# Transposing the attention output by DMA instead of TensorE in a fused attention and feed-forward kernel

## The chip, the cores and the metric

The kernel runs on one core of one Trainium2 chip. The metric is the device time of one execution in microseconds (us); the median over several runs is quoted. The span of an execution, from its first to its last instruction, is 1.7 to 1.8 us shorter than its time, so spans are compared with spans and times with times. TensorE is called PE, VectorE DVE, ScalarE ACT, GpSimd POOL; SP is the sync engine, whose sequencer issues DMAs in program order. PSUM is the memory that PE writes (`psum` in the profile). The granted clock is the share of full speed at which PE is let run. The chain of waits is followed back from the last instruction, at each step to what released it.

## The reference

Attention with a cosine-weighted linear kernel, 8 batches, 8 heads, 576 positions, head size 64. Its output, reordered to 4608 tokens x 512 channels, is the input of a feed-forward layer with a gate (512 to 1536 and back).

```python
def phi(x, c, s):                       # c, s: cos and sin of the position
    r = np.maximum(x, 0.0)
    return np.concatenate([r * c, r * s], axis=-1)
q_p, k_p = phi(q, cos_w, sin_w), phi(k, cos_w, sin_w)
kv  = einsum('bhsf,bhsd->bhfd', k_p, v);   z = sum(k_p, axis=2)
num = einsum('bhsf,bhfd->bhsd', q_p, kv)
den = einsum('bhsf,bhf->bhs', q_p, z)[..., None] + 1e-06
x   = (num / den).transpose(0, 2, 1, 3).reshape(4608, 512)
out = (gelu(x @ w_gate) * (x @ w_val)) @ w_out
```

## The kernel before

PE runs the feed-forward layer in nine blocks of 512 tokens. A block has 12 steps; each does the gate and value matmuls of 128 hidden columns (`gv_unit`, 8 matmuls of 512 columns) and a quarter of an output tile of the block before (`o_step`, 4 matmuls). In blocks 2 to 6 the attention of batch `blk + 1` (3 to 7) is threaded between them. A batch is 576 tokens and a block 512, so batch 3 fills the last 320 tokens of block 3 and the first 256 of block 4, while batch 7 fills only the last 64 of block 7 and all of block 8.

A batch goes through these units: `prep_step` makes the products of relu(q) and relu(k) with cos and sin on DVE, `cast_v` casts v on POOL, `turn_q` transposes the q products by DMA, `kv_unit` is the k-v product on PE, `nm_unit` makes the numerators and denominators of 128 tokens on PE and divides on DVE into `x_sb`, and `xt_unit` transposes that tile on PE and copies it with ACT into `xT`, which `gv_unit` reads as its moving operand. The product of gate and value is written by DVE into `hT`, which the output matmuls read.

```python
def nm_unit(b, t, bank=4):
    c0 = min(t * 128, S - 128)
    ps = psum[:, bank:bank + 2]
    ...                                   # 8 matmuls of 65 columns
    x = attn2.tile([128, 2, 4, D], BF16, name="x_sb")      # pool of 2 buffers
    nc.vector.tensor_scalar_add(den, nm[:, :, :, D], EPS)
    nc.vector.reciprocal(rec, den)
    nc.vector.tensor_tensor(x, nm[:, :, :, 0:D], ..., op=ALU.mult)
    bt[b, t] = x

def xt_unit(b, t, bank=6):
    x = bt.pop((b, t)).rearrange("p g h d -> p (g h d)")
    ps = psum[:, bank, 0:CT * 64].bitcast(BF16).rearrange("p (c n) -> p c n", c=CT)
    for ct in range(CT):                  # CT = 4
        nc.tensor.transpose(
            out=ps[:, ct, :], in_=x[:, ct * 128:(ct + 1) * 128], identity=ident)
    ...
    for blk, c, m in pieces(b * S + t * 128, n):           # a tile may span two blocks
        nc.scalar.copy(xT_block(blk)[:, :, c:c + m], ps[:, :, o:o + m])
        o += m

...
for blk in range(2, 9):
    b = blk + 1
    for jt in range(JT):                  # JT = 12 steps
        gv_unit(BLK * blk, BLK, jt)
        if b < B:
            if jt < 3:
                prep_step("kp", b, jt)
            if 1 <= jt < 5:
                cast_v(b, jt - 1, 1)
            if jt == 5:
                kv_unit(b)
                if b + 1 < B:
                    load_batch(b + 1)     # k, v of b+1 and q of b+2, on the sync queue
            if 6 <= jt < 6 + NT:          # NT = 5 tiles
                nm_unit(b, jt - 6)
            if jt >= 7:
                xt_unit(b, jt - 7)
            if b + 1 < B and jt >= 9:
                prep_step("qp", b + 1, jt - 9)
                if jt == 11:
                    turn_q(b + 1, 0, NP)  # two DMA transposes, on the sync queue
        o_step(blk - 1, jt)               # every third step also stores a tile
```

Of the kernel before, what the change touches and what calls it, by code (L numbers as in the profile page):

```python
# [10 lines left out]
BF16 = mybir.dt.bfloat16  # L11
# [5 lines left out]
def kernel(  # L17
# [14 lines left out]
    nc = tc.nc  # L32

    B, H, S, D = q.shape
# [16 lines left out]
    attn2 = ctx.enter_context(tc.tile_pool(name="attn2", bufs=2))  # L51
# [14 lines left out]
    def rows(t, b):  # L66
        return t[b].rearrange("(m i) (p j) d -> (i p) m (j d)", i=2, j=R)
# [3 lines left out]
    def load(eng, name, src, b, cuts=((0, NP),), j0=0, j1=R):  # L71
        if (name, b) not in staged:
            staged[name, b] = inp.tile(
                [128, NP, R * D], FP32, name=name, bufs=2 if name == "qf" else 1
            )
        js = slice(j0 * D, j1 * D)
        for m, n in cuts:
            eng.dma_start(
                out=staged[name, b][:, m:m + n, js], in_=rows(src, b)[:, m:m + n, js]
            )  # L80
# [48 lines left out]
    for i in range(2):  # L129
        t = consts.tile([128, NP, R, D + 1], BF16, name=f"vx{i}")  # L130
# [48 lines left out]
    def cast_v(b, m=0, n=NP, copy=nc.gpsimd.tensor_copy):  # L179
        copy(  # L180
            vx_tiles[b % 2][:, m:m + n, :, 0:D],
            staged["vf", b][:, m:m + n].rearrange("p m (j d) -> p m j d", j=R),
        )
# [48 lines left out]
    def turn_q(b, pair0, n):  # L232
        qt_tile(b)
        src = phi["qp", b]
        for i in range(2):
            nc.sync.dma_start_transpose(
                out=qT[b][i][:, pair0:pair0 + n].rearrange("f m (j p) -> f (m j) p", p=64),
                in_=src[64 * i:64 * i + 64, pair0:pair0 + n].rearrange(
                    "p m j f -> p (m j f)"
                ),  # L240
            )
# [3 lines left out]
    def kv_unit(b, groups=1):  # L245
        kp, vx = phi["kp", b], vx_tiles[b % 2]
        ps = psum[:, 4:6]
        kv = attn2.tile([128, NP, 2, D + 1], BF16, name="kv_sb")
        psv = ps[:, :, 0:NP * (D + 1)].rearrange("p i (m d) -> p m i d", m=NP)
        per = NP // groups  # L250
        for g in range(groups):
            for pair in range(g * per, (g + 1) * per):
                for j in range(R):
                    for i in range(2):
                        rr = slice(64 * i, 64 * i + 64)
                        nc.tensor.matmul(  # L256
                            psv[:, pair, i],
                            lhsT=kp[rr, pair, j, :],
                            rhs=vx[rr, pair, j, :],
                            start=(j == 0),  # L260
                            stop=(j == R - 1),
                        )
            nc.scalar.copy(kv[:, g * per:(g + 1) * per], psv[:, g * per:(g + 1) * per])
        kv_sb[b] = kv

    bt = {}
# [4 lines that stand above are left out]
        for h in range(H):  # L271
            nc.tensor.matmul(  # L272
                ps[:, h // 4, (h % 4) * (D + 1):(h % 4 + 1) * (D + 1)],
                lhsT=qT[b][h % 2][:, h // 2, c0:c0 + 128],
                rhs=kv_sb[b][:, h // 2, h % 2, :],
                start=True,
                stop=True,
            )
        nm = ps[:, :, 0:4 * (D + 1)].rearrange("p g (h d) -> p g h d", h=4)
        den = attn2.tile([128, 2, 4], FP32, name="den")  # L280
        rec = attn2.tile([128, 2, 4], FP32, name="rec")
        x = attn2.tile([128, 2, 4, D], BF16, name="x_sb")
        nc.vector.tensor_scalar_add(den, nm[:, :, :, D], EPS)
        nc.vector.reciprocal(rec, den)
        nc.vector.tensor_tensor(  # L285
            x,
            nm[:, :, :, 0:D],
            rec[:, :, :, None].to_broadcast([128, 2, 4, D]),
            op=ALU.mult,
        )  # L290
        bt[b, t] = x
# [3 lines left out]
    def xT_block(blk):  # L295
        if blk not in xT:
            xT[blk] = xtp.tile([128, CT, BLK], BF16, name="xT")
        return xT[blk]

    def pieces(c0, n):  # L300

        while n > 0:
            blk = c0 // BLK
            m = min(n, (blk + 1) * BLK - c0)
            yield blk, c0 % BLK, m
            c0, n = c0 + m, n - m
# [4 lines that stand above are left out]
        for ct in range(CT):  # L311
            nc.tensor.transpose(  # L312
                out=ps[:, ct, :], in_=x[:, ct * 128:(ct + 1) * 128], identity=ident
            )
        skip = 128 * (t + 1) - S if 128 * (t + 1) > S else 0
        n = 128 - skip
        o = skip
        for blk, c, m in pieces(b * S + t * 128, n):
            nc.scalar.copy(xT_block(blk)[:, :, c:c + m], ps[:, :, o:o + m])  # L319
            o += m  # L320


# [2 lines left out]
    def gv_unit(c0, n, jt):  # L325
        blk, cc = divmod(c0, BLK)
        xt = xT_block(blk)
        js = slice(jt * 128, (jt + 1) * 128)
        g_ps = next_bank()

        v_ps = g_ps[:, BLK // 2:] if n <= BLK // 2 else next_bank()
        for ps, w in ((g_ps, wg_sb), (v_ps, wv_sb)):
            for ct in range(CT):
                nc.tensor.matmul(  # L334
                    ps[:, 0:n],
                    lhsT=w[:, ct, js],
                    rhs=xt[:, ct, cc:cc + n],
                    start=(ct == 0),
                    stop=(ct == CT - 1),
                )  # L340
        gel = ffn.tile([128, BLK], FP32, name="gel")
        nc.scalar.activation(gel[:, 0:n], g_ps[:, 0:n], AF.Gelu)  # L342
        if blk not in hT:
            hT[blk] = ffn.tile([128, JT, BLK], BF16, name="hT")
        nc.vector.tensor_mul(hT[blk][:, jt, cc:cc + n], gel[:, 0:n], v_ps[:, 0:n])  # L345
# [31 lines left out]


    NT = 5
    def load_batch(b):  # L380
        load(nc.sync, "kf", k, b)
        load(nc.sync, "vf", v, b)
        if b + 1 < B:
            load(nc.sync, "qf", q, b + 1)


    probe = consts.tile([128, 1], FP32)
# [34 lines left out]
    kv_unit(0, 2)  # L422
    keep_warm(8)
    nm_unit(0, 0)
    nm_unit(0, 1, 0)
    keep_warm(8)
    xt_unit(0, 0)
    keep_warm(8)
    xt_unit(0, 1, 7)
    prep("qp", 0, 4, 6)  # L430
    prep("qp", 0, 6, 8)
    for jt in range(8):
        gv_unit(0, 256, jt)
        if jt == 0:
            turn_q_narrow(0, 4, 2)
            prep("qp", 0, 8, R)
        if jt == 1:
            turn_q_narrow(0, 6, 2)
        if jt == 2:
            nm_unit(0, 2)  # L440
        if jt == 3:
            turn_q_narrow(0, 8, 1)
        if jt == 4:
            nm_unit(0, 3)
            xt_unit(0, 2)
        if jt == 6:
            xt_unit(0, 3)
        if jt == 7:
            nm_unit(0, 4)
# [34 lines left out]
    def prep_step(name, b, i):  # L484
        prep(name, b, 3 * i, 3 * i + 3)

    def o_step(blk, i):
        o_part(4 * blk + i // 3, range(4 * (i % 3), 4 * (i % 3) + 4))
# [32 lines left out]
    for jt in range(4, JT):  # L521
# [12 lines left out]
        if jt < 11:  # L534
            o_step(0, jt - 1)
    load(nc.sync, "qf", q, 3)
    load_batch(3)
    nm_unit(2, 4)
    xt_unit(2, 3)
    o_step(0, 10)  # L540
# [6 lines left out]
    for blk in range(2, 9):  # L547
        b = blk + 1
        for jt in range(JT):
            gv_unit(BLK * blk, BLK, jt)  # L550
            if b < B:
                if jt < 3:
                    prep_step("kp", b, jt)
                if 1 <= jt < 5:
                    cast_v(b, jt - 1, 1)
                if jt == 5:
                    kv_unit(b)
                    if b + 1 < B:
                        load_batch(b + 1)
                if 6 <= jt < 6 + NT:  # L560
                    nm_unit(b, jt - 6)
                if jt >= 7:
                    xt_unit(b, jt - 7)
                if b + 1 < B and jt >= 9:
                    prep_step("qp", b + 1, jt - 9)
                    if jt == 11:
                        turn_q(b + 1, 0, NP)
            o_step(blk - 1, jt)
# [49 lines left out]
```

## Time and profile before

| | before |
|---|---|
| time, median of 3 runs | 345.82 us (345.78 to 345.93) |
| span of the profiled execution | 344.4 us |
| PE busy | 94%, granted clock 1.00 in the blocks |
| a block with a batch | 34.85 us |
| a block without | 31.1 us |

Lines of the code that the profile names: L334 gate and value matmuls, L365 output matmuls, L256 k-v, L272 numerators, L312 transposes of x, L319 copies into xT, L236 q transposes, L78 loads, L354 stores.

The page of the kernel before: its span, the busy time of each engine, and the chain of waits by engine and by line.

```profile
span 344.4 us, 6826 instructions
...
PE 324.5 (94%) x2700; PEld 180.9 (53%) x2738; DVE 192.4 (56%) x533; ACT 139.3 (40%) x281; POOL 30.5 (9%) x51
...
PE 88%; DVE 6%; DMA 2%; ACT 1%; issue 1%; SPq 0%; DVEq 0%; ACTq 0%
PE psum L334 52%; PE psum L365 25%; PE psum L256 3%; PE psum L272 3%; PE psum L312 2%; DMA vf<-in_v_dram 2%; DVE kp L148 1%; PE psum L207 1%; DVE x_sb L285 1%; DVE hT L345 1%; PE psum L579 1%; DVE vx_119 L180 1%; ACT xT L319 0%; DVE kp L158
...
L319 ACT COPY xT<-psum 128x512 bf16<-128x512 bf16 (+1 forms) x44 | 21.9, 508 | 24.4 <-PE psum L312 24.3
...
L312 PE MATMUL psum<-ident,x_sb 128*128 128x128 bf16 x160 | 15.5, 219 | 1.7 <-DVE x_sb L285 1.5
```

PE sets the pace of this kernel: it carries 88% of the chain, and the copies of ACT into xT alone waited 24.3 us for PE (the end of the L319 line). The transposes of x have 2.5% of the chain where it is printed with a decimal (2% here). Their 15.5 us "busy" is not what they cost: one is 219 ns long, so 160 of them end to end would be 35.0 us, and four that follow each other have 0.22 us of the chain. What they cost is read from the chain.

The chain in order of time, in the block of batch 4 (columns: start in us, duration in us, what). The k-v product, then steps 6 and 7:

```profile
142.69 1.27 PE psum L256 x72
...
143.96 0.16 issue
144.12 0.81 PE psum L365 x3
144.93 1.73 PE psum L334 x8
146.65 0.26 PE psum L272 x8
146.91 0.86 PE psum L365 x4
147.77 1.73 PE psum L334 x8
149.50 0.26 PE psum L272 x8
149.76 0.22 PE psum L312 x4
149.98 0.22 PE psum L365
```

A step is 1.73 of gate and value matmuls and 0.86 of output matmuls, 2.59 together. Around them stand k-v (1.27, with 0.16 of idle), a numerator (0.26) and a transpose group (0.22). 12 x 2.59 + 1.43 + 5 x (0.26 + 0.22) is 34.9, and the table of windows has 34.85 for the block from one step to the same step of the next block, so nothing else costs PE time there:

```profile
core 0: us, PE busy (x) PEld busy (x) DVE busy (x) ACT busy (x) POOL busy (x), PEclk, DMA share, GB/s
...
131.09:165.94 34.85, 34.48 (x271) 17.64 (x276) 22.37 (x64) 12.81 (x22) 2.50 (x4) 1.00 0.66 167
```

The sync queue at the turn of that block, from the timeline (start, duration, engine, line, operation). The two q transposes hold it for 8.5 us:

```profile
129.64 3.63 SPq L236 DMA_TRANSPOSE qT_2041<-qp  x1
133.36 4.77 SPq L236 DMA_TRANSPOSE qT_2042<-qp  x1
138.23 3.09 SPq L354 DMA_DIRECT2D out_dram<-o_sb  x4
141.41 0.55 SPq L78 DMA_DIRECT2D kf<-in_k_dram  x1
```

### The profile page before, as it was taken

Reading aid. Unit: us, or ns where it says so; the run is one execution under the profiler, and the core shown is the slowest. Engines: PE = TensorE matmul, PEld = TensorE weight load, DVE = VectorE, ACT = ScalarE, POOL = GpSimd, SP = SyncE. Lnnn points to the kernel's source line nnn. Section 1 sums busy time; section 2 is a strip of 40 time slices with the busy share of each in tenths; the row PEclk is TensorE's granted clock in tenths of the full one; section 3 lists DMA queues with packets and bytes.
Section 4 is the critical chain, followed back from the end, with each engine's and each line's share of the span. In section 5 each row is a group of like instructions: output and inputs, shape, how many; then the busy total and the mean of one; then the engine's idle time right before and its main releaser. Section 6 shows DMA issues by size and latency. Waiting matters only on the chain.

```text
span 344.4 us, 6826 instructions
## 1 busy us (share of the span) xinstructions
PE 324.5 (94%) x2700; PEld 180.9 (53%) x2738; DVE 192.4 (56%) x533; ACT 139.3 (40%) x281; POOL 30.5 (9%) x51
## 2 busy tenths in 40 slices
PE   3889998989899999999999999999999999999994
PEld 2778656755445554555455545554555444444443
DVE  5677865994792598258825882588355222322300
ACT  4667955533423443334324433343244333223221
POOL 1831022000200200020002000200000000000000
PEclk9999999999999999999999999999999999999999
DMA  7999984019569807990789079606711111211124
GB/s 285 260 273 305 240 296 163 2 36 371 207 86 237 317 4 107 227 340 0 99 203 370 3 86 216 236 0 92 139 32 33 30 30 38 50 35 30 32 62 91
DMA packets 47888, 48.81 MB, mean 142 GB/s; under 512 B 25200, under 2 KB 33136, under 8 KB 47856
## 3 DMA queue, kind: packets, MB, share of 16 engines
q1 hardware_dynamic: 38000, 34.64, 39.7%
q0 software_dynamic: 8480, 11.80, 14.4%
q10 hardware_dynamic: 1376, 1.93, 1.6%
q8 instruction: 21, 0.34, 0.4%
q14 instruction: 11, 0.09, 0.1%
HBM read 37.75 MB, written 9.44 MB: 137 GB/s over the span
## 4 chain that ended last, share of the span: by engine, by line
PE 88%; DVE 6%; DMA 2%; ACT 1%; issue 1%; SPq 0%; DVEq 0%; ACTq 0%
PE psum L334 52%; PE psum L365 25%; PE psum L256 3%; PE psum L272 3%; PE psum L312 2%; DMA vf<-in_v_dram 2%; DVE kp L148 1%; PE psum L207 1%; DVE x_sb L285 1%; DVE hT L345 1%; PE psum L579 1%; DVE vx_119 L180 1%; ACT xT L319 0%; DVE kp L158 0%; ACT gel L342 0%
## 5 line engine op out<-in xcount | busy, mean ns | idle before, releaser
L345 DVE TENSOR_TENSOR hT<-gel,psum 128x512 bf16<-128x512 f32 (+4 forms) x132 | 77.5, 590 | 127.3 <-PE psum L334 115.1
L342 ACT ACTIVATE gel<-psum 128x512 f32<-128x512 f32 (+4 forms) x132 | 68.5, 520 | 127.7 <-PE psum L334 121.6
L334 PE MATMUL psum<-xT,wg_sb 128*128 128x512 bf16 (+4 forms) x515 | 113.6, 339 | 2.4 <-ACT xT L319 1.4
L334 PE MATMUL psum<-xT,wv_sb 128*128 128x512 bf16 (+4 forms) x516 | 113.2, 339 | 0.6
L365 PE MATMUL psum<-wo_sb,hT 128*128 128x512 bf16 x407 | 104.3, 379 | 1.2 <-issue 0.8
L334 PEld LDWEIGHTS <-wg_sb 128*128 128x128 bf16 x528 | 48.4, 98 | 47.1 <-issue 2.1
L334 PEld LDWEIGHTS <-wv_sb 128*128 128x128 bf16 x528 | 49.0, 98 | 45.4
L365 PEld LDWEIGHTS <-hT 128*128 128x128 bf16 x420 | 38.7, 98 | 39.0
L319 ACT COPY xT<-psum 128x512 bf16<-128x512 bf16 (+1 forms) x44 | 21.9, 508 | 24.4 <-PE psum L312 24.3
L374 ACT COPY o_sb<-psum 128x512 f32<-128x512 f32 x35 | 20.5, 585 | 27.7 <-PE psum L365 26.6
L285 DVE TENSOR_TENSOR x_sb<-psum,rec 128x512 bf16<-128x512 f32 x40 | 27.7, 691 | 1.4
L148 DVE TENSOR_SCALAR qp<-qf,cos_t 128x256 bf16<-128x256 f32 x68 | 23.6, 347 | 0.0
L148 DVE TENSOR_SCALAR kp<-kf,cos_t 128x256 bf16<-128x256 f32 x63 | 21.7, 349 | 0.0
L148 DVE TENSOR_SCALAR qp<-qf,sin_t 128x256 bf16<-128x256 f32 x59 | 20.5, 347 | 0.0
L148 DVE TENSOR_SCALAR kp<-kf,sin_t 128x256 bf16<-128x256 f32 x57 | 20.0, 350 | 0.0
L312 PE MATMUL psum<-ident,x_sb 128*128 128x128 bf16 x160 | 15.5, 219 | 1.7 <-DVE x_sb L285 1.5
L180 POOL CAST vx_121<-vf 128x576 bf16<-128x576 f32 x12 | 7.5, 669 | 96.0 <-DMA vf<-in_v_dram 65.1
L207 PE MATMUL psum<-ident,qp 128*128 128x128 bf16 x108 | 9.2, 232 | 6.3 <-DVE qp L158 5.2
L180 POOL CAST vx_119<-vf 128x576 bf16<-128x576 f32 (+1 forms) x10 | 7.2, 765 | 65.6 <-DMA vf<-in_v_dram 65.6
L256 PEld LDWEIGHTS <-kp 64*128 64x128 bf16 x576 | 10.1, 95 | 5.4 <-issue 3.4
L312 PEld LDWEIGHTS <-x_sb 128*128 128x128 bf16 x160 | 10.0, 97 | 4.7 <-DVE x_sb L285 3.5
L207 PEld LDWEIGHTS <-qp 128*128 128x128 bf16 x108 | 7.3, 103 | 8.3 <-DVE qp L158 6.1
(88 smaller groups left out, 163.5 us busy)
## 6 DMA issues: line engine op xcount, KB each, us to landing
out_dram<-o_sb SPq DMA_DIRECT2D x70, 128.0 KB, 2.4
qf<-in_q_dram SPq DMA_DIRECT2D x5, 1152.0 KB, 11.6
kf<-in_k_dram SPq DMA_DIRECT2D x5, 1152.0 KB, 5.9
vf<-in_v_dram SPq DMA_DIRECT2D x5, 1152.0 KB, 9.2
qf<-in_q_dram POOLq DMA_DIRECT2D x2, 1152.0 KB, 16.3
kf<-in_k_dram POOLq DMA_DIRECT2D x2, 1152.0 KB, 11.4
vf<-in_v_dram POOLq DMA_DIRECT2D x2, 1152.0 KB, 11.8
wo_sb<-in_moe_w_out_dram POOLq DMA_DIRECT2D x2, 768.0 KB, 17.8
```

The costliest lines, as they stand in the source:

```text
L148: nc.vector.tensor_scalar(dst[:, m:m + n, j, part * D:(part + 1) * D], src[:, m:m + n, j], 0.0, (cos_t, sin_t)[part][:, j:j + 1], op0=ALU.max,
L180: copy(vx_tiles[b % 2][:, m:m + n, :, 0:D], staged["vf", b][:, m:m + n].rearrange("p m (j d) -> p m j d", j=R),)
L207: nc.tensor.transpose(out=views[m // per][:, m % per, j], in_=phi["qp", b][:, m, j0 + j, :], identity=ident,)
L256: nc.tensor.matmul(psv[:, pair, i], lhsT=kp[rr, pair, j, :], rhs=vx[rr, pair, j, :], start=(j == 0), stop=(j == R - 1),)
L285: nc.vector.tensor_tensor(x, nm[:, :, :, 0:D], rec[:, :, :, None].to_broadcast([128, 2, 4, D]), op=ALU.mult,)
L312: nc.tensor.transpose(out=ps[:, ct, :], in_=x[:, ct * 128:(ct + 1) * 128], identity=ident)
L319: nc.scalar.copy(xT_block(blk)[:, :, c:c + m], ps[:, :, o:o + m])
L334: nc.tensor.matmul(ps[:, 0:n], lhsT=w[:, ct, js], rhs=xt[:, ct, cc:cc + n], start=(ct == 0), stop=(ct == CT - 1),)
L342: nc.scalar.activation(gel[:, 0:n], g_ps[:, 0:n], AF.Gelu)
L345: nc.vector.tensor_mul(hT[blk][:, jt, cc:cc + n], gel[:, 0:n], v_ps[:, 0:n])
L365: nc.tensor.matmul(o_ps[i], lhsT=hT[blk][:, jt, tt * 128:(tt + 1) * 128], rhs=wo_sb[:, jt, :], start=(jt == 0), stop=(jt == JT - 1),)
L374: nc.scalar.copy(o_sb, o_ps.pop(i))
```

## The change

Its intent: take the 25 transpose groups of batches 3 to 7 off PE, which is the bottleneck, and give them to the DMA engines, which are idle a third of the time in a block with a batch (DMA share 0.66). A DMA takes longer to land (in the kernel before, the q transposes land 6.2 to 8.4 us after their issue, where a group on PE has 0.22 us and a copy into xT 0.51 us in the mean), so k-v and the numerators come one step sooner, there are four x buffers instead of two, and the loads of the next batch are spread over the block instead of being issued together after k-v. Batches 0 to 2 keep PE transposes.

```diff
-        x = attn2.tile([128, 2, 4, D], BF16, name="x_sb")
+        x = attn2.tile([128, 2, 4, D], BF16, name="x_sb", bufs=4)
...
+    def xt_dma(b, t):
+        x = bt.pop((b, t)).rearrange("p g h d -> p (g h d)")
+        o = max(128 * (t + 1) - S, 0)
+        for blk, c, m in pieces(b * S + t * 128, 128 - o):
+            nc.sync.dma_start_transpose(
+                out=xT_block(blk)[:, :, c:c + m], in_=x[o:o + m]
+            )
+            o += m
...
-    load_batch(3)
+    load(nc.sync, "kf", k, 3)
+    load(nc.sync, "vf", v, 3)
...
+                if jt == 0 and b + 1 < B:
+                    load(nc.sync, "qf", q, b + 1)
                 if jt < 3:
                     prep_step("kp", b, jt)
-                if 1 <= jt < 5:
-                    cast_v(b, jt - 1, 1)
-                if jt == 5:
+                if jt == 3 and b + 1 < B:
+                    load(nc.sync, "kf", k, b + 1)
+                if jt < 4:
+                    cast_v(b, jt, 1)
+                if jt == 4:
                     kv_unit(b)
                     if b + 1 < B:
-                        load_batch(b + 1)
-                if 6 <= jt < 6 + NT:
-                    nm_unit(b, jt - 6)
-                if jt >= 7:
-                    xt_unit(b, jt - 7)
+                        load(nc.sync, "vf", v, b + 1)
+                if 5 <= jt < 5 + NT:
+                    nm_unit(b, jt - 5)
+                    xt_dma(b, jt - 5)
```

More of the change, by code (lines that the diff above doesn't have):

```diff
@@ L379 @@
     NT = 5
-    def load_batch(b):
-        load(nc.sync, "kf", k, b)
-        load(nc.sync, "vf", v, b)
-        if b + 1 < B:
-            load(nc.sync, "qf", q, b + 1)
     probe = consts.tile([128, 1], FP32)
```

## The prediction

> **What bounds it now.** TensorE. On the profile page PE is busy 94% of the 344.4 us span at full granted clock, and the chain of waits is 88% PE, of which the transposes of the attention output are 2.5%. In the PE timeline a main-loop step without attention takes 2.59 us (8 gate/value matmuls 1.73, 4 output matmuls 0.86), with no gap. By the table of windows a block that also carries a batch takes 34.85 us: 12 x 2.59 = 31.1, k-v 1.5 (0.16 of it idle), five numerators of 0.26, five transposes of 0.22. The sum closes, so these blocks hide no other stall. DVE (22.4 of 34.85 us), ACT (12.8), POOL (2.5) and the DMA engines (share 0.66) have room.
>
> **Removed.** 25 groups of four transposes on PE. Each group starts 0.22 us before the output matmuls that follow it (149.60 to 149.82), all on the critical path: 25 x 0.22 = 5.5 us. The chain agrees: 2.5% of 344.4 us over 40 groups is 0.215 each. About 28 ACT copies of 0.5 us go too; ACT mostly waits for PE, so they are worth nothing.
>
> **Added.** 28 DMA transposes on the sync queue, 128 KB a tile. The trace has the operation for q: two of 590 KB, issued at 129.64 and 133.36, the second landing 7.1 us after its issue: 1.18 MB in 10.8 us, 110 GB/s; each holds the sequencer 3.6 to 4.8 us. Estimate for a tile: 1.2 us of transfer, 1 us of issue, 3 to 4 us to landing. [...]here TensorE spends 0.055 us a block in the chain[...].
>
> **Exposed?** The tightest deadline is batch 3: its first 2.5 tiles belong to the very next block. Tile 2 is computed in step 7, about 23 us into a block that will last 33.7; landed at 27, it has 6 us to spare. Later batches need fewer tiles early. Tile 0 is issued at 17 us, while the k and v loads drain (to about 20), and lands 2 to 4 us late, which four x buffers absorb. The transposed q lands 9.5 us into the block; its first use moves from 17.5 to 16. K-v now starts at 12.1 us; the k products end on DVE at 6, and v was cast in the block before. The sync queue is held 8 us by the q transposes, as now, so k and v loads are issued when they were; only q moves, with slack. So the moves and the spreading cost and gain nothing.
>
> **Prediction.** 345.8 - 5.5 = 340.3 us; 339.3 to 341.9 in 8 of 10. Faster by over 2% (under 338.9) 0.05, within 2% 0.92, slower 0.03.
>
> **What would show it.** The five batch blocks at 33.75 us instead of 34.85, blocks without a batch at 31.1; 100 fewer transposes on PE and their share of the chain down to about 1%; ACT busy down 14 us; no wait of gate/value matmuls for a DMA; x transposes landing in 3 to 6 us, the first of each batch slowest.
>
> **What would make it wrong.** DMA transposes of 128-row tiles much slower than those of q, so that block 3 waits for xT or DVE for an x buffer; the sync queue held in order by waits for x, so that stores come late and output buffers run out; q landing after numerator 0 is due[...]; or a hidden stall that the removed work was part of, which would give more than 5.5 us.

## The result, and the profile after

| | before | after |
|---|---|---|
| time, median (range) | 345.80 us (345.76 to 345.93) | 339.92 us (339.86 to 339.98) |
| ratio of after to before | | 0.9829 (95% interval 0.9812 to 0.9846) |
| span of the profiled execution | 344.4 us | 338.1 us |
| a block with a batch | 34.85 us | 33.73 us |
| a block without | 31.1 us | 31.1 us |
| ACT busy | 139.3 us | 125.6 us |

A ratio is the mean time of one kernel's fast runs over that of the other's of the same rounds, so it is not quite the ratio of the medians. The gain is 5.9 us or 1.7%: clear of noise, and below 2%.

In the kernel after, L334 is L343, L365 is L374, L354 is L363, and L326 is the new DMA transpose of x. The page after; PE is at the same 94% of a shorter span, and the copies into xT are down from 44 to 16:

```profile
span 338.1 us, 6688 instructions
...
PE 318.0 (94%) x2604; PEld 174.3 (52%) x2638; DVE 193.0 (57%) x533; ACT 125.6 (37%) x253; POOL 30.5 (9%) x51
...
PE 88%; DVE 5%; ACT 3%; DMA 2%; issue 1%; SPq 0%; DVEq 0%; ACTq 0%
PE psum L343 53%; PE psum L374 26%; PE psum L256 3%; PE psum L272 3%; DMA kf<-in_k_dram 2%; ACT kp L172 2%; DVE kp L148 1%; PE psum L207 1%; DVE x_sb L285 1%; PE psum L312 1%; DVE hT L354 1%; PE psum L587 1%; ACT xT L319 0%; ACT gel L351 0%
...
L319 ACT COPY xT<-psum 128x512 bf16<-128x512 bf16 (+1 forms) x16 | 8.2, 519 | 7.0 <-PE psum L312 6.9
...
```

The group of the remaining transposes, for batches 0 to 2, from the list of groups (it is too small now for the page):

```profile
L312 PE MATMUL psum<-ident,x_sb 128*128 128x128 bf16 x60 | 5.9, 220 | 1.7 <-DVE x_sb L285 1.5
```

The same stretch of the chain, k-v of batch 4 and the steps after it. Output matmuls now follow the numerator directly (142.51 + 0.26 = 142.77); the transpose group is gone and no wait has come in its place:

```profile
138.54 1.27 PE psum L256 x72
...
139.81 0.16 issue
139.97 0.81 PE psum L374 x3
140.78 1.73 PE psum L343 x8
142.51 0.26 PE psum L272 x8
142.77 0.86 PE psum L374 x4
143.63 1.73 PE psum L343 x8
145.36 0.26 PE psum L272 x8
```

The block in the table of windows (from mid-block to mid-block), 1.1 us shorter, which is five times 0.22:

```profile
128.18:161.92 33.74, 33.42 (x254) 16.50 (x256) 22.44 (x63) 10.11 (x17) 2.51 (x4) 1.00 0.85 190
```

The sync queue at the turn of that block, and the first transpose of x; then the DMA table's line for x (operation, count, median us from issue to landing). Each tile holds the queue 1.2 us or longer, a tile takes 2.3 to 8.6 us to land, the first of batches 3 to 6 in 7.8 to 8.6. There are 28 for 25 tiles, because three tiles span two blocks:

```profile
128.03 3.47 SPq L236 DMA_TRANSPOSE qT_2019<-qp  x1
131.60 4.83 SPq L236 DMA_TRANSPOSE qT_2020<-qp  x1
...
138.32 0.58 SPq L78 DMA_DIRECT2D qf<-in_q_dram  x1
...
144.37 1.60 SPq L326 DMA_TRANSPOSE xT<-x_sb  x1
```

```profile
xT<-x_sb SPq DMA_TRANSPOSE x28, 4.2
```

Five blocks times 1.12 us (34.85 to 33.73) are 5.6 of the 6.3 us between the spans. Of the rest, 0.44 us lies before the first gate matmul (it starts at 19.29 us before and at 18.85 after), where the two programs do the same work. The profiled execution of the kernel before took 346.18 us, 0.4 more than the median, which is why the spans differ by more than the times.

### The profile page after: what moved, and what is told of

It reads as the page before. It is cut to its first block, busy times and chain, and to the rows that moved or that the text cites. A ratio compares the mean times of both kernels' runs of the same rounds, so it can differ in the third digit from the quotient of the medians.

```text
span 338.1 us, 6688 instructions
## 1 busy us (share of the span) xinstructions
PE 318.0 (94%) x2604; PEld 174.3 (52%) x2638; DVE 193.0 (57%) x533; ACT 125.6 (37%) x253; POOL 30.5 (9%) x51
## 3 DMA queue, kind: packets, MB, share of 16 engines
q10 hardware_dynamic: 1376, 1.93, 1.7%
## 4 chain that ended last, share of the span: by engine, by line
PE 88%; DVE 5%; ACT 3%; DMA 2%; issue 1%; SPq 0%; DVEq 0%; ACTq 0%
PE psum L343 53%; PE psum L374 26%; PE psum L256 3%; PE psum L272 3%; DMA kf<-in_k_dram 2%; ACT kp L172 2%; DVE kp L148 1%; PE psum L207 1%; DVE x_sb L285 1%; PE psum L312 1%; DVE hT L354 1%; PE psum L587 1%; ACT xT L319 0%; ACT gel L351 0%; DVE rec L284 0%
## 5 line engine op out<-in xcount | busy, mean ns | idle before, releaser
L354 DVE TENSOR_TENSOR hT<-gel,psum 128x512 bf16<-128x512 f32 (+4 forms) x132 | 77.5, 590 | 121.0 <-PE psum L343 108.8
L351 ACT ACTIVATE gel<-psum 128x512 f32<-128x512 f32 (+4 forms) x132 | 68.5, 520 | 139.3 <-PE psum L343 131.2
L374 PE MATMUL psum<-wo_sb,hT 128*128 128x512 bf16 x398 | 103.0, 379 | 1.4 <-issue 0.8
L180 POOL CAST vx_119<-vf 128x576 bf16<-128x576 f32 (+1 forms) x10 | 7.3, 767 | 65.2 <-PE psum L374 31.1
L319 ACT COPY xT<-psum 128x512 bf16<-128x512 bf16 (+1 forms) x16 | 8.2, 519 | 7.0 <-PE psum L312 6.9
L263 ACT CAST kv_sb<-psum 128x520 bf16<-128x520 f32 (+1 forms) x10 | 5.1, 506 | 12.4 <-PE psum L256 12.4
L284 DVE RECIPROCAL rec<-den 128x8 f32<-128x8 f32 x40 | 8.1, 203 | 1.4
## 6 DMA issues: line engine op xcount, KB each, us to landing
vf<-in_v_dram POOLq DMA_DIRECT2D x2, 1152.0 KB, 11.8
```

The source lines that it names most:

```text
L180: copy(vx_tiles[b % 2][:, m:m + n, :, 0:D], staged["vf", b][:, m:m + n].rearrange("p m (j d) -> p m j d", j=R),)
L351: nc.scalar.activation(gel[:, 0:n], g_ps[:, 0:n], AF.Gelu)
L354: nc.vector.tensor_mul(hT[blk][:, jt, cc:cc + n], gel[:, 0:n], v_ps[:, 0:n])
L374: nc.tensor.matmul(o_ps[i], lhsT=hT[blk][:, jt, tt * 128:(tt + 1) * 128], rhs=wo_sb[:, jt, :], start=(jt == 0), stop=(jt == JT - 1),)
```

## The experiments

Twelve kernels were run, each in four or five timed executions; all gave the reference's result within its tolerance.

### Which part of the change does it: e1, e2, e3

My theory: all of the gain is PE time of the removed groups. Rival: the sooner k-v or the spread loads matter, either for themselves or because the transposes would not fit without them. e1 does the DMA transposes alone, e2 the schedule alone, e3 the buffers alone.

e1, against the kernel before (plus the function `xt_dma` and `bufs=4` as in the change):

```diff
                 if 6 <= jt < 6 + NT:
                     nm_unit(b, jt - 6)
-                if jt >= 7:
-                    xt_unit(b, jt - 7)
+                    xt_dma(b, jt - 6)
```

> The kernel before with one part of the change: x transposed by DMA right after each numerator (four x buffers), k-v still in step 5, loads still together after k-v. My theory (all of the gain is 25 groups of PE transposes at 0.22 us): 340.2 us, the five batch blocks at 33.73 us as in the changed kernel, nothing lost although tile 2 of batch 3 comes one step (2.85 us) later, because it had about 6 us to spare. Rival (k-v sooner and the spread loads are needed to make the DMA transposes fit): block 3 or DVE waits, and the time is 341.5 us or more.

Measured: 340.13 us (339.95 to 340.45), ratio to before 0.9831, blocks of 33.74 us, and no wait of PE for xT. The transposes alone are the gain; k-v sooner and spread loads add nothing that can be seen.

e2, against the kernel after (and two x buffers again):

```diff
-                    xt_dma(b, jt - 5)
+                if 6 <= jt < 6 + NT:
+                    xt_unit(b, jt - 6)
```

> The changed kernel with the DMA transposes taken out again: transposes on PE one step after each numerator, two x buffers, but k-v in step 4 and the loads spread. My theory: 345.8 us as before, blocks at 34.85 us. Rival (sooner k-v and spread loads have a worth of their own, for instance the 0.3 us that the 25 groups don't explain): 345.4 us or less.

Measured: 345.86 us (345.83 to 345.99), ratio 0.9996 (0.9983 to 1.0009), blocks of 34.86 us. The schedule by itself is worth nothing.

e3, against the kernel before:

```diff
-        x = attn2.tile([128, 2, 4, D], BF16, name="x_sb")
+        x = attn2.tile([128, 2, 4, D], BF16, name="x_sb", bufs=4)
```

> The kernel before with four x buffers instead of two and nothing else. The removed groups explain about 5.5 of the 5.9 us; the two traces also differ by 0.44 us before 19 us, where the program is the same but for the x buffers. If more x buffers, or the addresses that they shift, are the cause: 345.4 us and the first gate matmul at 18.85 us in place of 19.29. If it is chance of the one trace, or belongs to something else: 345.8 us.

Measured: 345.83 us (345.78 to 346.09), ratio 0.9996 (0.9983 to 1.0008); the first gate matmul starts at 19.19 us. So the 0.44 us between the first two traces is not owed to the buffers. The traces also say where the last 0.3 us of the 5.9 are not: from the first gate matmul to the end of the last matmul, before, e2 and e3 take 320.7 us (and e4, below, too), after and e1 315.1. That is 5.6 us, the 25 groups and nothing else. The rest lies before the first gate matmul, which starts between 18.84 and 19.29 us in all traces, and in the last stores; its cause stays open.

### Is it PE time? e4

e4, against the kernel after: the removed transposes back on PE, one step later than the numerator, into PSUM bank 6, read by nobody.

```diff
+                    shown[jt] = bt[b, jt - 5]
                     xt_dma(b, jt - 5)
+                if jt - 1 in shown:
+                    idle_transpose(shown.pop(jt - 1))   # the 4 transposes of xt_unit, no copy
```

> The changed kernel, all of it, plus the removed PE transposes put back one step after each numerator, their result used by nobody (no ACT copies). My theory: the 25 groups cost 0.22 us each, so 339.9 + 5.5 = 345.4 us, blocks at 34.83 us. Rival (the gain comes from the removed ACT copies or freed waits on PSUM bank 6, not from PE time): well under 343 us.

Measured: 345.68 us (345.56 to 345.77), ratio 0.9990 (0.9976 to 1.0003), blocks of 34.86 us. With the DMA transposes in place and the ACT copies still away, the PE transposes cost 5.8 us again. The rival that the ACT copies, or waits for them on bank 6, were the cause falls.

### What hides the slow landing: e5, e6

e5, against the kernel after: two x buffers.

```diff
-        x = attn2.tile([128, 2, 4, D], BF16, name="x_sb", bufs=4)
+        x = attn2.tile([128, 2, 4, D], BF16, name="x_sb")
```

> The changed kernel with two x buffers instead of four. In its trace tile 0 of a batch lands 8.5 us after its issue, because it queues behind the q, k and v loads. With two buffers the product of tile 2 on DVE must wait for tile 0 to land: at 119.2 us for batch 3 instead of starting at 115.6, and the numerators of tile 3 on PE then wait for DVE to free the PSUM banks, about 2.5 us a batch. If four buffers are what hides the slow landing: about 350 us (346 to 354). If the landing is not really in the way, for instance because PE has other work in its queue: 340 us.

Measured: 355.19 us (354.19 to 357.48), ratio 1.0287: slower by 15 us than with four buffers, and out of my range by 1.2 us. The totals of who waited for whom in e5 (engine, line, releaser: us in total, times, longest) show the two links of the expected wait:

```profile
DVE x_sb L285 <- DMA xT<-x_sb: 15.6, 5, 4.2
...
PE psum L272 <- DVE x_sb L285: 11.8, 5, 3.2
```

DVE waited 15.6 us in all for DMA to be done with an x before it wrote the next one there, and PE 11.8 us for DVE to be done with the PSUM banks of the numerator before. One of the five waits of PE (1.34 us, at tile 4 of batch 2) is in the kernel after as well. The other four, one in each of batches 3 to 6, are 2.25, 3.22, 2.31 and 2.67 us: 10.5 together, a mean of 2.6, near the expected 2.5. On the page the granted clock is 8 tenths in two slices, those at the waits of 3.22 and 2.67 us (149.8 to 158.6 and 229.1 to 237.9 us), and 9 or more elsewhere. Its mean over the run is 0.988, where the kernel after has 0.998: an estimate from these two means is 7 us at half clock, 3.5 us each, which costs up to 3.5 us more of PE time, the effect that e6 shows next. Together that is up to 14.0 of the 14.1 us by which the trace of e5 is longer from the first gate matmul to the last matmul. The buffers belong to the change as much as the transposes do.

e6, against the kernel after: tile 2 of batch 3 transposed after the q transposes of batch 4.

```diff
+                    if (b, jt) != (3, 7):
-                    xt_dma(b, jt - 5)
+                        xt_dma(b, jt - 5)
...
                         turn_q(b + 1, 0, NP)
+                        if b == 3:
+                            xt_dma(3, 2)
```

> The changed kernel with one DMA transpose (tile 2 of batch 3) put behind the two q transposes in the sync queue. It then issues near 136 us and lands near 141 us, while block 3 wants it at 129 us. If the deadline is real and the transposes' order in the queue is what keeps it: PE waits some 12 us for xT at the start of block 3, once, 352 us (349 to 354). If something else of slack hides it: under 345 us.

Measured: 355.05 us (354.40 to 355.62), ratio 1.0256: about 15 us lost to one late DMA, 3 us more than I expected and 1 us over my range. The wait is as expected. In the timeline of PE of e6, the first matmuls of block 3, and in brackets the idle time before them:

```profile
139.50 1.86 PE L343 MATMUL psum<-xT,wg_sb 128*128 128x512 bf16 x4 [12.83 <-issue]
```

And the table of windows of e6 (length; busy us and count of PE, PEld, DVE, ACT, POOL; granted clock; DMA share; GB/s), before the wait, with the wait, just after it, and later:

```profile
119.00:125.60 6.60, 6.60 (x39) 3.11 (x38) 5.41 (x17) 2.06 (x4) 1.94 (x4) 1.00 0.61 83
125.60:139.50 13.90, 1.07 (x5) 0.32 (x4) 2.58 (x9) 0.58 (x1) 0.00 (x0) 0.68 0.65 90
139.50:144.40 4.90, 4.89 (x12) 1.73 (x13) 1.22 (x4) 0.60 (x1) 0.00 (x0) 0.50 0.73 163
144.40:150.00 5.60, 5.60 (x27) 2.55 (x26) 4.23 (x14) 1.33 (x3) 0.00 (x0) 1.00 0.47 175
```

PE stands still for 12.83 us ("issue" only means that the profile has no event for what released it; the first half of tile 2 is issued at 136.48 and lands 2.9 us later, at 139.4). Then the clock column shows what I had not counted: the granted clock falls within the wait, to a mean of 0.68 over the 13.90 us that hold it, and for 4.90 us after it it is 0.50, and four matmuls take 1.86 us where 1.03 is usual. That is another 2.45 us (half of 4.90), and 12.8 + 2.45 makes 15.3, near the 15.1 us between e6 and the kernel after. How long the clock was at half can be estimated from the table: if it was either 1.00 or 0.50, a mean of 0.68 over 13.90 us is 8.9 us at half, so it fell some 4 us into the wait and was at half for 13.8 us in all. In e8, below, the same reckoning (0.86 over the 6.50 us with the wait, then 0.50 for 4.90 us) gives 6.7 us, and in e7 the slow matmuls last 3.4 us. So the 4.9 us are only what was left of a longer stretch at half clock when the wait ended.

### How much room is left: e7

e7, against the kernel after: every transpose of x done twice, first into a scratch tile.

```diff
+                    xt_twice(b, jt - 5)     # same DMA transposes into a scratch tile
                     xt_dma(b, jt - 5)
```

> The changed kernel with each of the 28 DMA transposes done twice, the first time into a scratch tile that nobody reads. Question: how much room have the sync queue and the DMA engines? The x transposes hold the queue about 8.3 us of a block of 33.7 and the q transposes 8.4, stores and loads about 7: doubled it is some 32 us, just under full. Tile 2 of batch 3 lands later, near 127 us with the deadline at 129. If the room is as large as that: 340 to 341 us. If the change already sits at the edge: 344 us or more.

Measured: 345.38 us (344.96 to 347.33), ratio 0.9993: all of the gain is lost again, and my expectation was wrong. Not tile 2 but the transposed q is late first. From the PE timeline of e7, numerator 0 of batch 6 and the gate matmuls after it (in e7 they are L354):

```profile
213.23 0.40 PE L272 MATMUL psum<-kv_sb,qT 128*128 128x65 bf16 x7 [2.12 <-DMA qT<-qp]
...
214.32 1.86 PE L354 MATMUL psum<-xT,wg_sb 128*128 128x512 bf16 x4
```

The blocks from one k-v to the next are 33.74, 34.82, 33.74 and 37.74 us long. The second of these has a wait of 0.9 us for q, the last a wait of 2.1 us for q and then, for 3.4 us (eight matmuls, 214.32 to 217.68), matmuls at half clock (1.86 for four where 1.03 is usual, as in e6 at a granted clock of 0.50). Reading the kernel after again with this in mind, for batch 4: the second q transpose is issued at 131.60 and lands 7.1 us later, at 138.7, and numerator 0 starts at 142.3. Its room is 3.6 us, and about as much for batches 5 to 7. For batch 3, whose q is transposed later, it is smaller still: issued at 100.31 (first line below, sync queue), landed 7.2 us later (second line, DMA table), at 107.5, and wanted at 108.6. That is 1.1 us, where the kernel before has 4.5:

```profile
100.31 4.65 SPq L236 DMA_TRANSPOSE qT_1628<-qp  x1
...
qT_1628<-qp SPq DMA_TRANSPOSE x1, 7.2
```

Tile 2 of batch 3 has more: it lands at 120.8 for a block that starts at 126.3, 5.5 us. The extra transposes stand before the q transposes in the same queue: for batch 6 those start at 202.65 us in e7, 4.4 us before k-v of that batch, and at 195.50 in the kernel after, 10.5 us before it.

### Taking it further: e8 to e12

The tiles 3 and 4 of batch 2 also belong to a block that starts much later. At the end of that stage PE waits 1.34 us for DVE before the numerator of tile 4; with a DMA transpose this numerator can move into block 2.

e8, against the kernel after:

```diff
         if 9 <= jt:
             xt_unit(2, jt - 9)
+        if jt == 11:
+            xt_dma(2, 3)
...
     load(nc.sync, "qf", q, 3)             # loads of batch 3, unchanged
...
-    nm_unit(2, 4)
-    xt_unit(2, 3)
     o_step(0, 10)
-    xt_unit(2, 4)
     o_step(0, 11)
...
+                if (b, jt) == (3, 1):      # in block 2
+                    nm_unit(2, 4)
+                    xt_dma(2, 4)
```

> The changed kernel taken further: tiles 3 and 4 of batch 2 also by DMA (they belong to block 3, so they have a whole block), and with that the numerators of tile 4 moved from the end of the stage, where PE waits 1.34 us for DVE, into step 1 of block 2. PE loses two transpose groups (0.44 us), the wait of 1.34 us and a second one near 0.4 us; DVE has less lead at k-v of batch 3, which may give 0.5 us back. By my theory that PE time is the clock: 337.7 us (337.3 to 338.4). If waits reappear in block 2: 339 us or more.

Measured: 346.46 us (345.59 to 347.28), ratio 1.0012: 6.5 us slower than the kernel after, a miss. The sync queue of e8 shows my mistake:

```profile
75.04 0.60 SPq L363 DMA_DIRECT2D out_dram<-o_sb  x1
90.06 1.29 SPq L326 DMA_TRANSPOSE xT<-x_sb  x1
91.45 0.53 SPq L78 DMA_DIRECT2D qf<-in_q_dram  x1
```

I had put a DMA that waits for x ahead of loads that wait for nothing. The queue issued them in order, so the loads stood still from 75.64 to 91.45 us, 15.8 us. DVE then waited 7.6 us for q, and PE, whose PSUM banks DVE was to empty, 6.4 us for DVE, with a granted clock of 0.50 for 4.9 us after it.

e9, against e8: the loads of batch 3 moved ahead of it in program order.

```diff
+        if jt == 8:
+            load(nc.sync, "qf", q, 3)
+            load(nc.sync, "kf", k, 3)
+            load(nc.sync, "vf", v, 3)
...
-    load(nc.sync, "qf", q, 3)
-    load(nc.sync, "kf", k, 3)
-    load(nc.sync, "vf", v, 3)
```

> e8 with one thing moved: the loads of q, k and v of batch 3 are issued before the DMA transpose of tile 3 of batch 2. In e8 that transpose waited in the sync queue for its x until 90 us and held the three loads (75.5 us in the changed kernel) back to 91.5 us, so DVE waited 7.6 us for q and PE 6.4 us for DVE. If that order is the whole reason for e8's loss: 337.7 us (337.3 to 338.4), as e8 was to give, and no wait for q. If tiles 3 and 4 or the moved numerators themselves do harm: 339.5 us or more.

Measured: 338.12 us (338.10 to 338.21), ratio to before 0.9777 (0.9764 to 0.9791), inside the range. The order was the whole loss. From k-v of batch 2 to k-v of batch 3 the trace is 2.26 us shorter than after; 0.4 us of it is given back in the last stores, whose landing was not looked into.

e10, against e9: tile 4 of batches 0 and 1 by DMA as well.

```diff
-            xt_unit(0, 4)
+            xt_dma(0, 4)
...
-            xt_unit(1, 4)
+            xt_dma(1, 4)
```

> e9 with tile 4 of batches 0 and 1 by DMA as well: both belong to a block that starts much later. Two more groups of 0.22 us off PE, so 0.4 us under e9: 337.3 us. If a start-up full of loads lets tile 4 of batch 0 land after 44 us, where the first fill wants it: e9 or more.

Measured: 337.75 us (337.61 to 338.11), ratio to before 0.9770 (0.9757 to 0.9783). Two groups more, 0.37 us less by the medians; the ranges touch, but the stretch from the first gate matmul to the last matmul is 0.38 us shorter in the trace too.

e11, against e10: the q transposes of batch 2 by DMA, its q products moved from the second of two short loops into the first, four short steps sooner (the expectation counts them as two).

```diff
     for jt in range(4):
         gv_unit(S, 256, jt)
         ...
+        if jt:
+            prep_step("qp", 2, jt - 1)
     nm_unit(1, 4)
     for jt in range(4):
         gv_unit(S + 256, 2 * BLK - S - 256, jt)
         if jt == 1:
             xt_dma(1, 4)
-        if jt:
-            prep_step("qp", 2, jt - 1)
+        if jt == 2:
+            turn_q(2, 0, NP)
...
-            turn_q_pe(2, 3 * (jt - 4), 3)
```

> e10 with the q transposes of batch 2 (36 on PE at 0.055 us, 12 copies on ACT and DVE) by DMA too, and the q products two steps sooner so that they land before numerator 0 near 77 us: issue near 60 us, landing near 72. PE loses 2.0 us and about 1 us of waits for those copies: 334.5 us (333.5 to 336). If the q products, moved into a stage where DVE is busy, hold up PE, or q lands after numerator 0: 336.5 us or more.

Measured: 337.53 us (337.29 to 337.83), ratio to before 0.9760 (0.9747 to 0.9773): no clear gain over e10, a miss. The q transposes start at 67.2 us, not near 60. PE lost 2 us of transposes and gained waits of 1.93 us (for an x behind the q products on DVE) and 1.37 us (for hT, likewise).

e12, against e11: the q products back in the second loop, one short step sooner than in e10, and half of the k products of batch 2 on ACT.

```diff
-        if jt:
-            prep_step("qp", 2, jt - 1)
     nm_unit(1, 4)
...
+        if jt < 3:
+            prep_step("qp", 2, jt)
         if jt == 2:
             turn_q(2, 0, NP)
...
-            prep_step("kp", 2, jt - 4)
+            prep_both("kp", 2, 3 * (jt - 4), 3 * (jt - 3))
```

> e11 with its new waits addressed. In e11 the q products, put into a busy stage, held DVE so that PE waited 1.9 us for an x and 1.4 us for hT, which ate the 2 us that the removed transposes gave. Here they come one step sooner than in e10 instead of two, and half of the k products of batch 2 go to ACT (9 of about 0.5 us each), so that DVE is ready for k-v near 72 us. The q transposes still issue near 67 us. If those two waits are what e11 lost: 335.0 us (334.4 to 336.2). If q now lands after numerator 0 wants it, or DVE is still behind at k-v: 336.8 us or more.

Measured: 338.88 us (338.82 to 339.86), ratio to before 0.9809 (0.9796 to 0.9823): slower than e10 and e11. The PE timeline of e12 at numerator 0 of batch 2:

```profile
79.59 0.40 PE L272 MATMUL psum<-kv_sb,qT 128*128 128x65 bf16 x7 [2.58 <-DMA qT<-qp]
```

PE now gets to the numerator sooner and waits 2.6 us for the transposed q. The q transposes start at 67.4 us in e12 and at 67.2 in e11, where PE came to the numerator so late that no wait for q shows. So as placed here batch 2 has no room for 12 us of q transposes, and what e11 removed from PE came back as a wait one way or the other. The best that I can recommend is e10: 337.75 us, 2.2 us under the change by the medians, and simpler than e11, from which it is not told apart.

## Why the prediction was right, point by point

- **The time.** Predicted 340.3 us (339.3 to 341.9), measured 339.92. The 5.5 us of the sum were 25 groups at 0.22. The blocks went from 34.85 to 33.73 us, predicted 33.75, and e4, which puts only the PE time back, costs 5.8. e1, e2 and e3 show that nothing else in the change moves the time. Some 0.3 us of the gain lies outside the stretch from the first gate matmul to the last matmul and is unexplained.
- **ACT copies worth nothing.** Right: ACT busy fell by 13.7 us (predicted 14), and e4, where the copies stay away, has the old time.
- **The costs of a DMA transpose.** About right for the sequencer: 1.2 us a tile, estimated 1. The landing was estimated at 3 to 4 us for a tile and 3 to 6 over all; it is 4.2 in the median, but 2.3 to 8.6. The tail is the first tile of each batch, behind the loads, as said, at the late end of what I said (3 or 4 plus 2 to 4, so 5 to 8) or just past it: 7.8 to 8.6 us in batches 3 to 6, and 2.3 us in batch 7, which has no loads ahead of it.
- **The room at each deadline.** Tile 2 of batch 3: 6 us predicted, 5.5 found, and e6 shows that the deadline is real. The transposed q: I gave it 6.5 us (landed at 9.5, wanted at 16); it has 3.6 for batches 4 to 7 and 1.1 for batch 3. I had counted the block from 131.09, which lies in its second step already; counted from its first, q lands 12.4 us in and is wanted at 16. The same slip put the end of the k products at 6 us; in block 2 it is 10.5, 1.7 us before k-v. None of it was exposed, so the total held, but with 1.1 us left that was luck and not reckoning: the deadline that I called the tightest, tile 2 of batch 3, was not.
- **The moves gain and cost nothing.** Right for the time (e1 and e2). But they are not idle: k-v one step sooner gives x a step and takes one from q, which is the shorter of the two. e1, without it, has the same blocks.
- **Four buffers absorb the slow tile.** Right, and larger than I would have said: without them the change loses 9 us against the kernel before (e5).

## What to carry to other kernels

When one engine has no gaps, the worth of removing work from it is the count times its cost in the chain of waits, and it can be taken from one step of the timeline (here 25 x 0.22 = 5.5 us, of 5.9 measured). What then decides is not how long the replacement takes but whether it lands before its reader comes: work out the room of every deadline that shares the queue, including those the change does not mention, and count it from the right start. In a DMA queue that issues in order never put a DMA that waits for data ahead of loads that wait for nothing: in e8 it held three loads back by 15.8 us and cost 8.3 us against e9. And a wait on TensorE can cost more than its length, because the clock may fall with it: here it fell at waits of 2.1 us (e7), 2.7 and 3.2 us (e5), 6.4 us (e8) and 12.8 us (e6), though not at one of 0.9 us (e7) and not at two of 2.3 us (e5).

## What the traces show of transposes by DMA

- In a stream a tile of four blocks of 128x128 costs 0.22 us of PE time (0.055 a block, though one transpose is 219 ns long in the trace). By DMA it holds the sync queue 1.2 us or longer (0.3 a block), though it lands only after 2.3 to 8.6 us.
- In the kernel after, with the DMA engines busy in full both times (share 1.00 and 1.01), the q transposes moved 130 GB/s and the loads 368. The transposes of x, which moved alone from 119.9 to 120.3 us, reached 225:

```profile
110.00:112.00 2.00, 2.00 (x18) 1.06 (x17) 0.88 (x2) 1.11 (x2) 0.00 (x0) 1.00 1.01 368
132.00:136.00 4.00, 4.00 (x20) 1.77 (x19) 3.41 (x12) 1.78 (x3) 0.00 (x0) 1.00 1.00 130
```

- In the sequencer a q transpose of 64 partitions and 4608 columns (590 KB) took 3.5 to 4.8 us, and a tile of x of 128 partitions and 512 columns (128 KB) 1.2 us or longer, up to 2.0. A part of a tile, 64 partitions and the same 512 columns, took 1.2 us too: half the rows took as long, and nine times the columns three to four times as long. It decides what else that queue can do.
